# Forgetting attention and a SwiGLU block: q and k of the first three batches through GpSimd's DMA queue with a cast on the way

## The chip, the cores and the metric

The kernel runs on one core of a Trainium2 chip. The time is that of one execution on the device, in microseconds (us); lower is better. Each core has TensorE (PE in the profile; its weight loads are PEld), VectorE (DVE), ScalarE (ACT), GpSimd (POOL) and SyncE (SP), and DMA queues that the engines issue into. TensorE's results land in PSUM, of which there are eight banks, and are read from there by DVE or ACT.

## What is computed

Eight batches, eight heads, 576 tokens, head size 64; then a feed-forward block over all 4608 tokens (model width 512, inner width 1536).

```python
scores = scale * np.matmul(q, k.transpose(0, 1, 3, 2))
cum = np.cumsum(np.log(np.clip(f, 0.0001, 1.0)), axis=-1)
scores = np.where(causal, -1000000000.0, scores + cum[:, :, :, None] - cum[:, :, None, :])
attn = softmax(scores)                                  # over the last axis
x = np.matmul(attn, v)                                  # (B, H, S, D) -> (B*S, H*D)
g = x @ w_gate
out = (g * sigmoid(g) * (x @ w_val)) @ w_out
```

All inputs and the output are float32; the kernel computes its matmuls in bfloat16.

## The kernel before

**Attention.** Two heads make a pair, four pairs a batch. `QK` holds, for eight pairs at a time, q and k turned so that the head's 64 channels lie on partitions 0 to 63 and the tokens along the row; four further partitions hold the decay in parts, so that one matmul of 68 rows gives scores with decay. For each head, `score` writes four groups of score columns to PSUM (the first of them, i = 0, needs only tokens 0 to 255), `expo` takes the exponential on ACT, `mask` zeroes the upper triangle on GpSimd, `weigh` multiplies by v on TensorE, `invert` and `scale` normalise on DVE, `flip` and `put` turn the result into `xT`, the feed-forward block's input.

**Feed-forward block.** For each tile of tokens, 12 inner blocks: `gate` with `wg`, tanh on ACT, two DVE operations, `gate` with `wv` between them, then `project` with `wo`. Batch 0's 576 tokens are two tiles (256 and 320), the rest are tiles of 512.

**Loads before the change.** v comes by SyncE in float32 and is cast, mostly on GpSimd. The weights come by GpSimd with a cast to bfloat16 in the transfer, 384 columns (or three inner blocks) at a time: `weights`, L708 for gate and value, L705 for out. For q and k there are three ways:

- Batch 0, `first_queries` (L500): SyncE loads float32 in two token halves (0 to 255, then 256 to 575; L473), TensorE turns them in float32 against a float32 identity (`turn_x`, L485), ACT and DVE copy them into `QK` with the cast (`straighten_x`).
- Batches 1 and 2, `queries` (L521): SyncE loads 96 partitions of 2 heads x 6 tokens (L408) into unused places of `xT`, or of `wo` for pairs 4 and 5; `cast_qk` casts them into one of four `BF` buffers on ACT, DVE or GpSimd; `turn` (L418) turns one token of both heads at a time, 128 columns of `BF`, whose last 32 partitions are zero; `straighten` copies into `QK`.
- Batches 3 to 7: `narrow` casts q and k from memory to memory by GpSimd, and SyncE's transposing DMA (L435) brings them into `QK`.

**Decay.** f is loaded on ACT's queue in two parts; for each part clip, Ln, a running sum and four scaled remainders follow (L314 to L334), and `row` (L352) moves them into `QK`'s decay rows by SyncE's queue.

**Order of the work.** A planner (`Plan.run`, L66) runs once when the program is built. Each operation has a key, an earliest time, needs and an estimated cost; the planner plays the engines forward and emits, on each, the ready operation with the lowest key. The result is a fixed order per engine: at run time each engine takes its instructions in that order and waits at each for what it needs. The constants at the end of the file (`W_AT`, `Q1_AT`, `KEY_X`, ...) shift these keys and earliest times. Where the planner sees TensorE idle between 2 and 40 us with a free bank, it puts in a filler matmul (`dummy`, L813) whose result nobody reads. Score and turn results can borrow the feed-forward block's four banks until `BORROW`.

Helpers record many operations under one line: L295 is a copy or cast on ACT, L297 one on DVE or GpSimd, L337 a fill.

Of the kernel before, what the change touches and what calls it, by code (L numbers as in the profile page):

```python
# [23 lines left out]
class Op:  # L24
    def __init__(self, eng, fn, after, take, use, key, ready, dma, late):
        self.eng, self.fn, self.take, self.use = eng, fn, take, take + use
        self.key, self.ready, self.dma, self.late = key, ready, dma, late
        self.after = [a for a in after if a is not None]
        self.next, self.wait = [], 0
        self.start = self.done = None  # L30


class Plan:
# [9 lines left out]
    def op(self, eng, fn, after=(), take=(), use=(), key=0.0, ready=0.0, dma=None, late=0.0):  # L43
        o = Op(eng, fn, list(after), list(take), list(use), key, ready, dma, late)
        for b in o.use:
            b.left += 1
        self.ops.append(o)
        return o
# [17 lines left out]
    def run(self, idle=None):  # L66
# [12 lines left out]

        def push(at, kind, o):  # L80
            nonlocal seq
            seq += 1
            heapq.heappush(events, (at, seq, kind, o))
# [4 lines left out]
        while left:  # L88
# [4 lines left out]
            while events and events[0][0] <= t + 1e-9:  # L93
                _, _, kind, o = heapq.heappop(events)
                if kind in ("queue", "dma"):
                    busy_rings = [r for r in rings.values() if r]
                    for r in busy_rings:
                        r[0][0] -= (t - moved) * (0.6 if len(busy_rings) > 1 else 1.0)
                        while r and r[0][0] < 1e-6:
                            over, n = r.pop(0)  # L100
                            if r:
                                r[0][0] += over
                            n.done = t + 1.0
                            push(n.done, "end", n)
                            push(n.done + n.late, "done", (n, None, False))
                    moved = t
                    if kind == "queue":
                        rings["POOL" if o.ran == "POOL" else "HW"].append([o.dma, o])
                    busy_rings = [r for r in rings.values() if r]
                    if busy_rings:  # L110
                        push(t + min(r[0][0] for r in busy_rings) / (0.6 if len(busy_rings) > 1 else 1.0), "dma", None)
# [80 lines left out]
def kernel(ctx, tc, q, k, v, f, w_gate, w_val, w_out, out):  # L192
# [39 lines left out]
    BF = [sb(f"BF{i}", [P, QT, 2, D], BF16) for i in range(4)]  # L232
# [13 lines left out]
    def part(r):  # L246
        return wo[:, KF // 4 * r : KF // 4 * (r + 1)].rearrange("p a b -> p (a b)")

    lf, zero, cum, r1 = [xT[:BH, r, : 2 * S].bitcast(F32) for r in range(4)]
    dec = [xT[:BH, r, N_TOK - 2 * S :].rearrange("p (w s) -> p w s", w=2) for r in range(4)]  # L250
    nat = {"nat": [xT[:QP, r, N_TOK - 2 * S - 4 * QT * D : N_TOK - 2 * S].bitcast(F32).rearrange("p (h x) -> p h x", h=2) for r in range(KD)],
           "natw": [part(r)[:QP].bitcast(F32).rearrange("p (h x) -> p h x", h=2) for r in range(4)]}

    TX, PX = (2, 4), (HALF // 2, (S - HALF) // 4)
    natx = [[OT[r].rearrange("p (h x y) -> p x h y", h=2, x=2) for r in range(FB)],
            [xT[: PX[1], r, N_TOK - 2 * S - 8 * TX[1] * D : N_TOK - 2 * S].bitcast(F32).rearrange("p (h x y) -> p x h y", h=2, x=2) for r in range(FB)]]
    ident32 = consts.tile([P, P], F32, name="ident32")
# [3 lines left out]
        {"f": 4, "s": 2, "o": 1, "t": 1, "pt0": NPT0, "pt": NPT, "vb": NVB, "nv": NNV, "nat": KD, "natw": 4, "bf": 4,  # L261
# [78 lines left out]
    o_one = op(("POOL", 0.1), fill, warm, 1.0, key=-20)  # L340
    o_wln = op(("ACT", 1.5), lambda e: nc.scalar.activation(warm, warm, AF.Ln), after=[o_one], key=-18)
    o_id = op(("POOL", 0.8), lambda e: make_identity(nc, ident[:, :]), key=-19)
    o_zero = op(("DVE", 0.55), fill, zero, 0.0, key=-18)
    o_dec = [op(("DVE", 0.25), fill, dec[r][:, 0 if r else 1], 1.0, key=-17) for r in range(4)]
    o_i32 = op(("DVE", 0.4), lambda e: nc.vector.tensor_copy(ident32, ident), after=[o_id], key=-16)
    o_bf = [op(("POOL", 0.75), lambda e, i: fill(e, BF[i][QP:], 0.0), i, key=60, ready=22.0) for i in range(4)]

    def row(e, r, c):
        n = (FB, FIRST * FB)[c]
        for p0, p1, x in ((0, FB, CUTS[c]),) if c == 0 else ((0, FB, CUTS[c]), (FB, FIRST * FB, slice(0, S))):  # L350
            if p0 < p1:
                E[e].dma_start(  # L352
                    out=QK[D + r : D + r + 1, p0:p1, :, x].rearrange("o b (j w) s -> o (b j) w s", w=2),
                    in_=dec[r][2 * p0 : 2 * p1, :, x],
                )
# [3 lines left out]
    for c in range(2):  # L359
        x, kc, d = CUTS[c], (-15, CHAIN)[c], (256, 320)[c] / 960  # L360
        o = op(("DVE", 0.15 + d), clip, c, after=[o_f[c]], key=-16)
        o = op(("ACT", 0.2 + d), log, c, after=[o, o_wln], key=-16)
# [8 lines left out]
        o_row.append([op((ROWQ[c], (0.5, 0.9)[c] if FIRST > 1 else 0.5), row, r, c, after=[a, o_dec[r]] + o_chain[r : 4 * c : 4], key=ROW_KEY[c] + r,  # L371
                         dma=0.2) for r, a in enumerate((o_up, o_hi, o_mid, o_lo))])
# [19 lines left out]
    o_warm = op(("ACT", 1.4), lambda e: nc.scalar.activation(warm, lf[:1, :1], AF.Exp), after=[o_ln], key=-14)  # L392
# [14 lines left out]
    def ld_qk(e, p, nm, b):  # L407
        nc.sync.dma_start(out=nat[b.pool][b.i], in_=srcs[nm][2 * p : 2 * p + 2].rearrange("h (p t) d -> p h (t d)", t=QT))  # L408

    def cast_qk(e, bn, bb):  # L410
        dst, src = BF[bb.i][:QP].rearrange("p t h d -> p h t d"), nat[bn.pool][bn.i].rearrange("p h (t d) -> p h t d", d=D)
        copy(e, dst, src)

    def turn(e, bb, bt):
        src = BF[bb.i].rearrange("p t h d -> p t (h d)")
        t = ps(bt).bitcast(BF16)
        for n in range(QT):
            nc.tensor.transpose(t[:, n * QP : n * QP + P], src[:, n], ident)  # L418

    def straighten(e, p, x, a, bt):  # L420
        dst = QK[:D, hqk[p].i, 2 * a + x, :S].rearrange("p (c n) -> p c n", n=QT)
        src = ps(bt).bitcast(BF16)[a * D : (a + 1) * D, :S].rearrange("p (n c) -> p c n", n=QT)
# [30 lines left out]
    def values(b, n, key, after=(), ready=0.0):  # L453
        bv = Buf("nv")
        o = op(("SP", SPi), ld_v, b, n, bv, take=[bv], key=key, dma=1.6 if n < NB - 1 else 0.8, after=after,
               ready=ready, late=LATE if b >= FIRST else 0.0, tag=("ldv", b, n))
# [10 lines left out]
    a_ready, x_turned = {}, []  # L467
    prev_narrow = {}
    wo_free = []

    def ld_x(e, p, nm, x, half):
        n, lo = TX[half], HALF * half
        nc.sync.dma_start(  # L473
            out=natx[half][p][:, x],
            in_=srcs[nm][2 * p : 2 * p + 2, lo : lo + n * PX[half]].rearrange("h (p t) d -> p h (t d)", t=n),
        )

    def turn_x(e, p, half, xs, bt):
        m = PX[half]
        c = 0  # L480
        for x in xs:
            for h in range(2):
                for y in range(TX[half] // 2):
                    o = ps(bt)[:, c : c + TX[half] // 2 * m].rearrange("p (n y) -> p y n", y=TX[half] // 2)[:, y]
                    nc.tensor.transpose(o, natx[half][p][:, x, h, P * y : P * y + P], ident32[:m, :m])  # L485
                c += TX[half] // 2 * m

    def straighten_x(e, p, half, xs, t, bt):
        n, lo = TX[half] // 2 * PX[half], HALF * half
        q = QK[:D, p, :, lo : lo + 2 * n]  # L490
        src = ps(bt)[t * D : (t + 1) * D, : len(xs) * 2 * n]
        if half:
            dst = q[:, xs[0] :: 2].rearrange("p h (n t) -> p h n t", t=2)[:, :, :, t]
            src = src.rearrange("p (h n) -> p h n", h=2)
        else:
            dst = q.rearrange("p (h x) (n t) -> p x h n t", x=2, t=2)[:, :, :, :, t]
            src = src.rearrange("p (x h n) -> p x h n", x=2, h=2)
        copy(e, dst, src)

    def first_queries(p):  # L500
        strs = []
        for half in range(2):
            key = KEY_X[half] + 5 * p
            lds = [op(("SP", SPi), ld_x, p, nm, x, half, key=KEY_L[half] + 5 * p + x, dma=(0.67, 0.71)[half], ready=X_AT[half],
                      tag=("ldx", p, half)) for x, nm in enumerate("qk")]
            for xs in ([0, 1],) if half == 0 else ([0], [1]):
                bt = Buf("t", ("f", 30.0), ("s", 12.0))
                o3 = op(("PE", 4 * (0.15, 0.1)[half]), turn_x, p, half, xs, bt, after=[lds[x] for x in xs] + [o_i32], take=[bt],
                        key=key, tag=("turnx", p, half))
                x_turned.append(o3)  # L510
                for t in range(2):
                    strs.append(op({"ACT": (0.7, 0.5)[half], "DVE": (0.7, 0.5)[half]}, straighten_x, p, half, xs, t, bt,
                                   after=[o3] + strs[:1], take=[] if strs else [hqk[p]],
                                   use=[bt] + ([hqk[p]] if strs else []), key=key, tag=("strx", p, half)))
            for j in range(2):
                if half:
                    q_ready[2 * p + j] = strs + o_row[0] + o_row[1]
                else:
                    a_ready[2 * p + j] = strs + o_row[0]
# [354 lines left out]
```

The softmax here doesn't subtract the row's maximum and nothing guards it: scores larger than these inputs give would overflow.

## Time and profile before

| | |
|---|---|
| median of 4 runs | 407.27 us (407.2 to 407.58) |
| the profiled execution, its own time | 406.87 us |
| its span, first to last instruction | 405.2 us |
| TensorE busy | 392.5 us, 97% |
| TensorE weight loads | 232.0 us, 57% |
| DVE busy | 230.8 us, 57% |
| ACT busy | 225.1 us, 56% |
| GpSimd busy | 128.9 us, 32% |
| SyncE's DMA queue (q1), GpSimd's (q0) | 38.8 MB and 10.6 MB, 46.7% and 16.6% of the DMA engines' span |
| read from memory, written | 38.3 MB, 15.8 MB |

Times inside the profile count from the span's start. A busy TensorE is not TensorE at its best: matmuls overlap, their ends are modelled, and the clock may be reduced (PEclk, 1.00 is full). A DMA share over 1 comes from packets of two queues that overlap on one DMA engine. The chain of waits follows the work that ended last back to what released it, so a long DMA entry in it is a time in which the end of the kernel waited for that load.

### The profile page before, as it was taken

What the parts mean: (1) busy time and instruction counts of PE and PEld (TensorE: products, weight loads), DVE (VectorE), ACT (ScalarE), POOL (GpSimd) and SP (SyncE); (2) the same over time, 40 slices, a digit from 0 to 9 for tenths busy, and PEclk for the clock granted to TensorE, in tenths of its full rate; (3) what the DMA queues carried; (4) which work ended last, traced back from release to release, by engine and by line L of the source; (5) the groups of instructions that cost most, each with busy time, mean ns of one, the idle gap of its engine ahead of it and who ended that gap; (6) DMA issues with size and microseconds to landing.
All of it is one profiled execution on the core that took longest, in us unless ns stands there. A gap on an engine that the chain in (4) does not pass through costs nothing.

```text
span 405.2 us, 8557 instructions
## 1 busy us (share of the span) xinstructions
PE 392.5 (97%) x3166; PEld 232.0 (57%) x3211; DVE 230.8 (57%) x452; ACT 225.1 (56%) x457; POOL 128.9 (32%) x357
## 2 busy tenths in 40 slices
PE   8979999999999999999999999999999999999996
PEld 6748878655554555556556555565664444444542
DVE  7525988646772477337643675267743761770850
ACT  6558978747762665466636665566763322322321
POOL 4938655443350333234415432533330000000000
PEclk9979999999999999999999999999999999999999
DMA  8999999047952985899699879975202002002002
GB/s 201 185 216 217 223 228 211 30 148 173 184 96 81 193 163 112 151 196 163 105 156 196 154 138 148 146 155 119 48 28 79 0 2 104 0 2 103 2 10 82
DMA packets 105818, 50.12 MB, mean 124 GB/s; under 512 B 87920, under 2 KB 100656, under 8 KB 105456
## 3 DMA queue, kind: packets, MB, share of 16 engines
q1 hardware_dynamic: 99312, 38.80, 46.7%
q0 software_dynamic: 6304, 10.62, 16.6%
q8 instruction: 25, 0.41, 0.4%
q10 hardware_dynamic: 160, 0.15, 0.2%
q14 instruction: 17, 0.14, 0.1%
HBM read 38.34 MB, written 15.78 MB: 134 GB/s over the span
## 4 chain that ended last, share of the span: by engine, by line
PE 86%; DMA 7%; SPq 3%; DVE 2%; issue 1%; ACT 1%; ACTq 0%; DVEq 0%
PE ps L712 42%; PE ps L727 23%; PE ps L580 10%; PE ps L611 7%; DMA xT<-in_k_dram 4%; SPq L435 2%; DMA QK<-dec_d 2%; PE ps L635 2%; PE ps L418 1%; DMA xT<-in_f_dram 1%; DVE QK L297 0%; PE ps L813 0%; SPq L352 0%; DVE xT L321 0%; DVE xT L328 0%
## 5 line engine op out<-in xcount | busy, mean ns | idle before, releaser
L712 PE MATMUL ps<-xT,wv 128*128 128x512 bf16 (+3 forms) x467 | 111.9, 358 | 0.8
L712 PE MATMUL ps<-xT,wg 128*128 128x512 bf16 (+3 forms) x465 | 111.5, 359 | 0.7
L716 ACT ACTIVATE th<-ps 128x512 f32<-128x512 f32 (+3 forms) x120 | 66.5, 555 | 72.3 <-PE ps L712 70.7
L588 ACT ACTIVATE PT<-ps 128x384 bf16<-128x384 f32 (+2 forms) x192 | 93.0, 507 | 23.9 <-PE ps L580 14.1
L720 DVE SCALAR_TENSOR_TENSOR th<-th,ps 128x512 f32<-128x512 f32 (+3 forms) x120 | 75.5, 629 | 53.4 <-ACT th L716 53.0
L727 PE MATMUL ps<-wo,hh 128*128 128x512 bf16 (+1 forms) x427 | 104.3, 379 | 0.9
L723 DVE TENSOR_TENSOR hh<-th,ps 128x512 bf16<-128x512 f32 (+3 forms) x120 | 76.1, 634 | 14.6 <-PE ps L712 2.8
L597 POOL TENSOR_SCALAR_AFFINE_SELECT PT<-PT 128x128 bf16<-128x128 bf16 (+1 forms) x192 | 53.1, 279 | 83.3 <-ACT PT L588 78.2
L580 PE MATMUL ps<-QK 68*128 68x320 bf16 (+4 forms) x448 | 72.5, 263 | 1.6 <-DMA QK<-xT 1.0
L712 PEld LDWEIGHTS <-wv 128*128 128x128 bf16 x480 | 45.1, 98 | 35.7 <-issue 0.4
L727 PEld LDWEIGHTS <-hh 128*128 128x128 bf16 (+1 forms) x444 | 41.8, 98 | 41.4 <-issue 1.2
L712 PEld LDWEIGHTS <-wg 128*128 128x128 bf16 x480 | 45.1, 98 | 35.3
L597 POOL TENSOR_SCALAR_AFFINE_SELECT PTa<-PTa 128x256 bf16<-128x256 bf16 x64 | 25.7, 410 | 82.4 <-ACT PTa L588 76.3
L731 ACT ACTIVATE ot<-ps 128x512 f32<-128x512 f32 (+1 forms) x37 | 22.1, 597 | 51.5 <-PE ps L727 51.3
L618 DVE RECIPROCAL rc<-ps 128x5 f32<-128x5 f32 (+2 forms) x64 | 12.3, 191 | 63.7 <-PE ps L611 63.3
L611 PEld LDWEIGHTS <-PT 128*128 128x128 bf16 x768 | 38.3, 97 | 17.7 <-POOL PT L597 1.1
L611 PE MATMUL ps<-VB,PT 128*128 128x65 bf16 x768 | 45.4, 193 | 0.1
L580 PEld LDWEIGHTS <-QK 68*128 68x128 bf16 x448 | 34.8, 98 | 12.3 <-issue 1.8
L588 ACT ACTIVATE PTa<-ps 128x384 bf16<-128x384 f32 x64 | 30.7, 491 | 15.8 <-PE ps L580 15.6
L625 DVE TENSOR_TENSOR xn<-ps,rc 128x320 bf16<-128x320 f32 x56 | 27.5, 491 | 1.8
L295 ACT ACTIVATE QK<-ps 64x576 bf16<-64x576 bf16 (+2 forms) x31 | 19.3, 628 | 9.7 <-DVE QK L297 7.9
L297 POOL CAST VB<-natv 128x512 bf16<-128x512 f32 (+1 forms) x38 | 23.2, 620 | 4.7 <-DMA natv<-in_v_dram 4.7
(54 smaller groups left out, 196.8 us busy)
## 6 DMA issues: line engine op xcount, KB each, us to landing
out_dram<-ot SPq DMA_DIRECT2D x35, 256.0 KB
natv<-in_v_dram SPq DMA_DIRECT2D x32, 256.0 KB
qk_d<-in_q_dram POOLq DMA_DIRECT2D x5, 576.0 KB, 6.2
qk_d<-in_k_dram POOLq DMA_DIRECT2D x5, 576.0 KB, 9.6
xT<-in_q_dram SPq DMA_DIRECT2D x6, 288.0 KB
xT<-in_k_dram SPq DMA_DIRECT2D x6, 288.0 KB
wg<-in_moe_w_gate_dram POOLq DMA_DIRECT2D x4, 384.0 KB, 9.9
wv<-in_moe_w_val_dram POOLq DMA_DIRECT2D x4, 384.0 KB, 11.5
```

Source lines behind the costliest of these rows:

```text
L297: E[e].tensor_copy(dst, src)
L580: nc.tensor.matmul(s[:, c : c + w], QK[:KR, hqk[p].i, 2 * j + 1, kt * P : (kt + 1) * P], QK[:KR, hqk[p].i, 2 * j, q0 : q0 + w], start=True ...
L588: nc.scalar.activation(place(h, i)[:, OFFS[i] : OFFS[i] + c], ps(bs)[:, :c], AF.Exp, scale=0.125)
L597: nc.gpsimd.affine_select(out=d, in_=d, pattern=pat, compare_op=ALU.is_ge, fill=0.0, base=0, channel_multiplier=-1,)
L611: nc.tensor.matmul(o[:, lo : lo + D + 1], pt[:, c : c + P], VB[hvb[b].i][:, kt, hb, : D + 1], start=first and n == 0, stop=last and n == l ...
L625: nc.vector.tensor_mul(XN[bx.i][:, qb : qb + nq, j], o, r)
L712: nc.tensor.matmul(ps(bf)[:, :n], w[:, ko, fc * P : (fc + 1) * P], xT[:, ko, t0 : t0 + n], start=(ko == 0), stop=(ko == KD - 1))
L716: nc.scalar.activation(TH[bt.i][:, :n], ps(bf)[:, :n], AF.Tanh, scale=0.5)
L720: nc.vector.scalar_tensor_tensor(out=t, in0=t, scalar=1.0, in1=ps(bf)[:, :n], op0=ALU.add, op1=ALU.mult)
L723: nc.vector.tensor_mul(HH[:, bh.i, lo : lo + n], TH[bt.i][:, :n], ps(bf)[:, :n])
L727: nc.tensor.matmul(ps(bf)[:m, :DM], HH[:, hs[fc].i, lo : lo + m], wo[:, fc, :], start=(fc == 0), stop=(fc == KF - 1))
L731: nc.scalar.activation(OT[bo.i][:m], ps(bf)[:m, :DM], AF.Copy, scale=0.5)
```

## The change

All 24 tensors-of-a-pair of batches 0 to 2 (q and k of 12 pairs) are loaded by GpSimd's queue, cast to bfloat16 in the transfer, 96 partitions of 2 heads x 6 tokens each. `first_queries`, its two token halves, the float32 identity, `cast_qk` and the `BF` buffers go. `turn` now takes two neighbouring tokens of one head at a time: 96 partitions of 128 columns, six per tensor, straight from the loaded tile. There are eight places in `xT` and eight in `wo`; batch 1 uses those in `wo`, so all of `w_out`'s loads now wait for batch 1's last turn. `row` is cut into three steps (batch 0's first part, batch 0's second part, batch 1). The planner's picture of the two DMA rings is refined (a starting GpSimd ring takes nearly all), its costs of loads are changed, and the constants at the end of the file are new, which moves many instructions on every engine. In the built program the number of fillers goes from 95 to 59. On GpSimd's queue the eight loads of batch 0 stand ahead of the first six weight transfers.

```diff
 class Op:
-    def __init__(self, eng, fn, after, take, use, key, ready, dma, late):
+    def __init__(self, eng, fn, after, take, use, key, ready, dma, late, pk):
+        self.pk = pk
...
+        def share(busy):
+            if rings["POOL"] and rings["POOL"][0][1] is None:
+                return [1.0 if r is rings["POOL"] else 0.1 for r in busy]
+            return [0.6, 0.65] if len(busy) > 1 else [1.0]
...
                     if kind == "queue":
-                        rings["POOL" if o.ran == "POOL" else "HW"].append([o.dma, o])
+                        r = rings["POOL" if o.ran == "POOL" else "HW"]
+                        if o.ran == "POOL" and not r:
+                            r.append([1.5, None])
+                        r.append([o.dma, o])
...
-    BF = [sb(f"BF{i}", [P, QT, 2, D], BF16) for i in range(4)]
...
+    def places(t, lo, n):
+        return [t[:QP, lo + i * 2 * QT * D : lo + (i + 1) * 2 * QT * D].rearrange("p (h t) -> p h t", h=2) for i in range(n)]
+
+    nat = {"nat": [a for r in range(KD) for a in places(xT[:, r], N_TOK - 2 * S - 4 * QT * D, 2)],
+           "natw": places(wo.rearrange("p a b -> p (a b)"), 0, 8)}
...
-    o_one = op(("POOL", 0.1), fill, warm, 1.0, key=-20)
+    o_one = op(("DVE", 0.1), fill, warm, 1.0, key=-20)
-    o_id = op(("POOL", 0.8), lambda e: make_identity(nc, ident[:, :]), key=-19)
+    o_id = op(("POOL", 0.8), lambda e: make_identity(nc, ident[:, :]), key=KEY_Q + 3.5)
-    o_i32 = op(("DVE", 0.4), lambda e: nc.vector.tensor_copy(ident32, ident), after=[o_id], key=-16)
-    o_bf = [op(("POOL", 0.75), lambda e, i: fill(e, BF[i][QP:], 0.0), i, key=60, ready=22.0) for i in range(4)]
...
     def ld_qk(e, p, nm, b):
-        nc.sync.dma_start(out=nat[b.pool][b.i], in_=srcs[nm][2 * p : 2 * p + 2].rearrange("h (p t) d -> p h (t d)", t=QT))
-
-    def cast_qk(e, bn, bb):
-        dst, src = BF[bb.i][:QP].rearrange("p t h d -> p h t d"), nat[bn.pool][bn.i].rearrange("p h (t d) -> p h t d", d=D)
-        copy(e, dst, src)
-
-    def turn(e, bb, bt):
-        src = BF[bb.i].rearrange("p t h d -> p t (h d)")
-        t = ps(bt).bitcast(BF16)
-        for n in range(QT):
-            nc.tensor.transpose(t[:, n * QP : n * QP + P], src[:, n], ident)
+        nc.gpsimd.dma_start(out=nat[b.pool][b.i], in_=srcs[nm][2 * p : 2 * p + 2].rearrange("h (p t) d -> p h (t d)", t=QT))
+
+    def turn(e, bn, bt):
+        src, t, n = nat[bn.pool][bn.i], ps(bt).bitcast(BF16), 0
+        for h in range(2):
+            for y in range(QT // 2):
+                nc.tensor.transpose(t[:, n : n + QP], src[:, h, P * y : P * y + P], ident[:QP, :QP])
+                n += QP
 
     def straighten(e, p, x, a, bt):
-        dst = QK[:D, hqk[p].i, 2 * a + x, :S].rearrange("p (c n) -> p c n", n=QT)
-        src = ps(bt).bitcast(BF16)[a * D : (a + 1) * D, :S].rearrange("p (n c) -> p c n", n=QT)
+        dst = QK[:D, hqk[p].i, x::2, :S].rearrange("p h (n y t) -> p h n y t", n=QP, t=2)[:, :, :, :, a]
+        src = ps(bt).bitcast(BF16)[a * D : (a + 1) * D, :2 * S // 2].rearrange("p (h y n) -> p h n y", h=2, n=QP)
         copy(e, dst, src)
...
                 kk = key + 2 * x
-                o1 = op(("SP", SPi), ld_qk, p, nm, bn, take=[bn], key=kk, dma=1.1, after=x_turned,
-                        ready=max(ready, release(p) - SLACK) + 0.9 * x,
-                        tag=("ldqk", p))
-                o2 = op(copier(QT * 2 * D, False), cast_qk, bn, bb,
-                        after=[o1] + o_bf, take=[bb], use=[bn], key=kk, tag=("cast", p))
-                if p in WPAIRS:
-                    wo_free.append(o2)
-                o3 = op(("PE", mm(*[P] * QT)), turn, bb, bt, after=[o2, o_id], take=[bt], use=[bb], key=kk,
-                        tag=("turn", p))
+                o1 = op(("POOL", 0.35), ld_qk, p, nm, bn, take=[bn], key=kk, dma=0.74,
+                        ready=max(ready, release(p) - SLACK) + 0.3 * x, tag=("ldqk", p), late=(0.0, LATE0, LATE)[b])
+                o3 = op(("PE", mm(*[QP] * QT)), turn, bn, bt, after=[o1, o_id], take=[bt], use=[bn], key=kk, tag=("turn", p))
+                if b == 1:
+                    wo_free.append(o3)
...
     for p in range(FB):
-        first_queries(p)
+        queries(p, KEY_Q + 4 * p)
...
-W_AT = [9.0, 14.5, 11.3, 31.6]
-WO_AT = [35.2, 23.3, 56.0, 39.0]
-Q1_AT = [12.3, 35.1, 34.2, 53.1]
-V1_AT = 34.2
-CHAIN = 16.8
+W_AT = [-2.8, -18.4, -0.5, 15.6]
+WO_AT = [28.1, 28.3, 50.7, 57.5]
+Q1_AT = [24.1, 27.1, 27.5, 39.5]
+V1_AT = 28.1
+CHAIN = 30.6
...
-FREE = 128.1
+FREE = 87.7
...
-BORROW = 24.0
+BORROW = 33.9
+KEY_Q = -17.9
```

## The prediction, made before the changed kernel was run

> **What bounds the kernel now.** I read the busy shares first. TensorE is busy 97% of the span, and in the page's slices only the opening is visibly thin. Lines 1 and 2 of the page, then the stages of the opening (TensorE's busy time and count, granted clock, DMA share, GB/s):
>
> ```profile
> PE 392.5 (97%) x3166; PEld 232.0 (57%) x3211; DVE 230.8 (57%) x452; ACT 225.1 (56%) x457; POOL 128.9 (32%) x357
> PE   8979999999999999999999999999999999999996
> ...
> 15.00:20.00 5.00, 4.73 (x63) 1.00 1.24 239
> 20.00:25.00 5.00, 2.55 (x28) 0.98 1.34 206
> 25.00:30.00 5.00, 4.43 (x24) 0.50 1.24 232
> 30.00:35.00 5.00, 5.00 (x44) 0.83 1.12 201
> 35.00:40.00 5.00, 5.00 (x79) 1.00 1.16 226
> ```
>
> Busy hides two things: fillers (L813, work that nobody needs) and a clock at half from about 24.8 to 31.7. So I used a ledger: the matmuls in instruction order, each at its issue interval, fillers and early turns (L485) left out. The intervals come from runs of equal matmuls: four of 512 columns in 0.86 us give 0.216 each, other widths in proportion, nothing under 0.055; 24 products P·V (L611) in 0.89 us give 0.037. The whole kernel comes to 377.8 us. What the clock shows beyond the ledger is TensorE's loss so far. The chain of waits gives the clock at each mark:
>
> ```profile
> 13.38 8.57 DMA xT<-in_k_dram
> 21.96 5.84 DMA xT<-in_k_dram
> 27.94 0.78 PE ps L485 x4
> 29.93 2.29 PE ps L712 x12
> ...
> 72.17 0.65 PE ps L727 x3
> ```
>
> First gate (L712, start 28.77): ledger 4.4, loss 24.4. First turn of batch 1 (L418, 37.98): ledger 10.8, loss 27.2. First projection (72.17): ledger 45.1, loss 27.1. End (405.2): 377.8, loss 27.4. **So everything TensorE loses is lost before 38 us; the other 367 us are dense.** The loss is made by the two long waits above: SyncE's loads of batch 0's second token half, in flight beside the weights, keep the last turns of pairs 2 and 3 back, and behind them, in order, all other TensorE work.
>
> **What the Trainium skill says.** "DMA: Bandwidth & Descriptors", Queues, rings and completion order: all queues share 16 engines, each of which goes round-robin between queues, packet by packet. The trace agrees: a 160 KB load took 8.57 us from issue to landing beside weights. The same page, SWDGE vs HWDGE vs iDMA: a cast in the transfer can only be issued by GpSimd, which writes the descriptors itself. So each load costs GpSimd time; the trace has 0.53 us for a two-index load and 0.77 to 1.07 for weights. "TensorE: Matmul & The Clock Gate", Part 1: the clock goes to half after an idle window of about 3.4 us and comes back after a busy one. The trace agrees roughly: half clock for 6.8 us after a stage only 51% busy.
>
> **The change, part by part.**
> *Removed.* 16 casts (8 on DVE at 0.55 to 0.65, 2 on ACT at 0.84, 6 on GpSimd at 0.82: 11 us over three engines), four zero fills of 0.73 on GpSimd, GpSimd's two decay scalings (0.94 and 1.14, now on ACT at an estimated 0.45, like its Ln), 32 SyncE issues of about 0.46. None lies on TensorE's dense path; they count only in the opening.
> *TensorE.* 96 turns of 128 columns become 144 of 96, at 0.055 each: +2.6 us in the ledger, now 380.4. They include batch 0's, which the 48 float32 turns did before (outside the ledger, in idle time).
> *Data.* 24 loads of 288 KB (144 KB written) go through GpSimd's queue. The packet records show 192-packet transfers costing what weights cost per packet: 512 weight packets moved in 2.0 us alone, so 0.76 each. Batch 0's eight stand ahead of the weights in the same ring, so nothing of the weights can delay them; that is the core of the change. A first weight packet moved 1.7 us after the issue began, and a starting ring moved 126 packets per us: first load 2.5, five loads (pairs 0, 1 and q of pair 2, all that stands before the first score) by about 10, eight by 13, six weight transfers by 25, the last two by 29. SyncE keeps only v and the decay rows; rows of batch 0 are issued from about 6.3 to 9.6 (before 7.1 to 10.35).
> *First score.* Two issues, a fill and the identity put TensorE's first filler at 3.2 (before 1.46). By the fillers' own spacing the clock became full 6.3 us after the first one; say 9.5. In the order 48 fillers (0.23 cold, 0.11 warm) and 30 turns precede the first score: about 22 fillers and 12 turns cold, 26 × 0.11 + 18 × 0.06 + 0.1 = 4.0 warm: 13.5 us. Before: 14.96. First exponential 13.9.
> *ACT then sets the pace.* Almost all of batch 0's attention now precedes the FFN. Before the gate stand, in ACT's order, 8 early exponentials (0.491), heads 0 to 4 (0.597 + 0.488 + 0.437 = 1.52 each), two of head 5 and 3 straightenings (0.644): 3.9 + 7.6 + 1.1 + 1.9 = 14.6. 28.5, plus mask and product: first gate about 29.4, no earlier than before. But the ledger there is 12.7, not 4.4. Batch 0's last exponential ends 18.4 us after the first, 32.3; its last product stands at ledger 15.9 and runs at about 33.5: loss 17.6.
> *After that.* From first to 24th tanh, ACT's operations sum to 32.9 us and DVE's to 33.6, against 37.3 in the ledger: TensorE leads again. Before, ACT was 84 to 88% busy in 30 to 70 us and TensorE lost nothing. I add 1.1 for small waits: loss 18.7.
> *Late next.* Batch 1's turns come at 17.7 + 18.7 = 36.4 and later; their loads are issued from about 26 and land at about 30: hidden by 5 us. w_out is issued behind batch 1's last turn, 34.5 + 18.7 = 53.2, and GpSimd waits there with the masks behind it; the exponentials for those come later in the order too. Three issues by 55.6, a fourth at about 58; landing took 8.0 to 11.0 before: 66 to 69, against the first projection at 50.7 + 18.7 = 69.4. Hidden, with little to spare; up to 2 us if not.
> *Sum.* 380.4 + 18.7 = 399.1 of span, against 405.2. The profiled execution took 406.87, 1.67 more than its span, and the median of the runs is 0.40 above that: 401.2, say **401.3 us**.
>
> **Unknown costs, both ends.** A 192-packet load on GpSimd: 0.53 (nearest row) to 1.07 (longest issue seen); taken 0.55. At 0.8 the ten before the gate add 2.5 to GpSimd's 27 us and make it the pacer. A 96-row turn: 0.04 (columns alone) to 0.083 (busy time each of L418's): -1.4 to +2.7 us over batches 1 and 2; taken 0.055. The first use of GpSimd's queue at 0.8 instead of 9.5 us: the first issue took 0.2 longer than the next; I take nothing, with 0 to 2 us as bounds, and 2 us earlier never helps since ACT paces. A fuller ring: before, five weight transfers were issued ahead of the first landing without a stall; now 14 could be issued by 12.6, and a stall would cost 0 to 2.
>
> **Rivals.**
> *B, part of it is given back:* GpSimd's issues at 0.8, or w_out late, cost 2 to 5 us: 403 to 406, say 404.5. For it: GpSimd has 27 us of work before the gate that waits for it at 29. Against: masks of neighbouring heads overlap in the trace.
> *C, hidden anyway:* the later loads and their transposes (DMA 80 to 90% busy in many slices to 280 us) hold TensorE to its old times: no change, 407.3. Against: zero loss from 38 us on.
> *D, slower, by the clock:* from 14 to 29 TensorE has 10 us of ledger in 15.5, 65%, with no fillers after the first products, where the filler-padded stage before it was 95% busy. If the clock drops for the attention stage, 10 becomes 20 us (gate at 34) and the recovery costs what it cost before, 6.8 at half, 3.4: 8 us on top, 409. It decides at 6.1 us lost, or 12.2 us of dense work at half clock. Against: the drop in the trace followed 51% busy with whole idle microseconds; here gaps are fractions of one.
> That the change doesn't do what it says is no rival: in the built order the 24 loads stand on GpSimd, bf16, before the weights.
>
> **How the numbers follow.** Forecast A 0.60 (own range 398.5 to 404), B 0.17, C 0.05, D 0.13, anything else slower 0.05. A change of 0.2% (0.8 us) is about what a measurement of this kernel can tell from none. Faster: A and B, 0.77. Same: C and B's edge, 0.06. Slower: D and the rest, 0.17. Low end 397.5: A with 0.04 turns and first gate 1 us earlier. High end 408.5: B, C and a milder D, leaving about 0.1 above.
>
> **What would show it.** Right: no load of k in the chain of waits after 15 us; first score near 13.5, first gate near 29.4 but with batch 0's attention nearly done; ACT close to 100% from 14 to 31; clock full in 20 to 35; dense TensorE from 34; first projection near 69. Wrong: first score after 16, half clock after 15, GpSimd without idle before the gate or issues of 0.8 and more, TensorE waiting for w_out or for batch 1's loads.

## The result: no change, and where the profile puts the time

The changed kernel takes 407.5 us in the median (36 runs), the kernel before, run beside it, 407.2 us (55 runs). The ratio is 1.0001, with a 95% interval from 0.9986 to 1.0015: no difference that can be measured, where 401.3 us and a faster kernel had been forecast. Some executions are several us longer at a lower granted clock; all ratios leave these out, and so are not quite the quotients of the medians. The profiled execution of the changed kernel took 406.62 us, its span 404.6 us (before: 406.87 and 405.2).

The page of the changed kernel, TensorE's busy time, its 40 slices and its granted clock:

```profile
PE 383.9 (95%) x3130; PEld 225.1 (56%) x3175; DVE 230.4 (57%) x444; ACT 220.7 (55%) x448; POOL 133.2 (33%) x369
PE   5659999999999999999999999999999999999996
PEclk9959999999999999999999999999999999999999
```

The same stages of the opening as were shown of the kernel before (stage, then length, TensorE's busy time and count, granted clock, DMA share, GB/s):

```profile
15.00:20.00 5.00, 3.38 (x45) 1.00 1.27 193
20.00:25.00 5.00, 0.42 (x7) 0.62 1.29 192
25.00:30.00 5.00, 5.00 (x43) 0.50 1.27 196
30.00:35.00 5.00, 4.85 (x79) 0.85 1.34 179
35.00:40.00 5.00, 4.37 (x60) 1.00 1.29 224
```

The emptiest stage, 20 to 25 us, has become emptier (2.55 to 0.42 us of work), and a half clock is still there, now from 21.2 to 31.5 us. TensorE's waits from 12 to 45 us (engine, line and tile, what it waited for: us in all, times, longest) and the chain of waits name what is late:

```profile
PE ps L528 <- DMA QK<-xT: 6.3, 2, 4.6
```

```profile
14.02 10.72 DMA QK<-xT
24.74 0.14 issue
24.88 1.55 PE ps L528 x8
```

The two long waits for `xT<-in_k_dram` are gone. In their place stands one wait of 10.72 us for `QK<-xT`: the decay rows of batch 0's second token part, tiny transfers on SyncE's queue, issued by `row` (L354) at about 14 us and landed at 24.74. The timeline shows that they were not alone (start, length, engine and line, operation; the bracket gives the idle time before and what ended it):

```profile
10.08 0.73 SPq L443 DMA_DIRECT2D natv<-in_v_dram  x1
10.91 1.51 SPq L354 DMA_DIRECT2D QK<-xT  x2
12.47 0.44 SPq L443 DMA_DIRECT2D natv<-in_v_dram  x1
13.00 2.43 SPq L354 DMA_DIRECT2D QK<-xT  x3
24.52 0.61 POOL L302 CAST VB<-natv 128x512 bf16<-128x512 f32 x1 [3.89 <-DMA natv<-in_v_dram]
24.88 1.55 PE L528 MATMUL ps<-QK 68*128 68x192 bf16 x8 [4.58 <-DMA QK<-xT]
```

v's blocks 4 and 3 of batch 0 (L443) were issued in between, at 10.1 and 12.5 us, and block 3 landed only at about 24.5: from issue to landing block 4 took over 8 us, the last row 10.7 and block 3 12. What moved in those ten microseconds, by queue (packets, MB, share of 16 engines; q0 is GpSimd's queue, q1 SyncE's):

```profile
q0 software_dynamic: 1933, 1.44, 92.1%
q1 hardware_dynamic: 1776, 0.48, 34.6%
```

A packet here is one record of the profile, one piece of a transfer. The two queues moved nearly one packet for one packet. A packet of GpSimd's loads writes 768 bytes, one of v 256. SyncE's queue got 178 packets, or 48 KB, per us. From 2 to 4 us, with almost nothing beside it, it had moved 1545 packets and 0.39 MB, 195 KB per us, its start included. Before the change the same ten microseconds had 836 packets of SyncE with 0.71 MB, because its loads of q and k came in packets of 1024 bytes. GpSimd's queue moved 2006 there, so equal counts are not seen in that kernel; SyncE's queue had gaps (62 packets from 20 to 23 us).

The first gate starts at 36.4 us (28.8 before), the first projection at 75.3 (71.2 before). From the first projection to the end it is 329.3 us, against 334.0 before: the dense part became shorter, since more of the attention is done ahead of it, but the opening became longer by 4.1, and the two nearly cancel: 0.6 us of span is left, less than the executions of one kernel differ by.

### The profile page after: what moved, and what is told of

It is laid out like the page before. It is cut to its first block, busy times and chain, and to the rows that moved or that the text cites. A ratio compares the mean times of both kernels' runs of the same rounds, so it can differ in the third digit from the quotient of the medians.

```text
span 404.6 us, 8424 instructions
## 1 busy us (share of the span) xinstructions
PE 383.9 (95%) x3130; PEld 225.1 (56%) x3175; DVE 230.4 (57%) x444; ACT 220.7 (55%) x448; POOL 133.2 (33%) x369
## 4 chain that ended last, share of the span: by engine, by line
PE 85%; DVE 6%; DMA 3%; issue 2%; ACT 2%; POOL 1%; SPq 0%; DVEq 0%; ACTq 0%; POOLq 0%
PE ps L660 42%; PE ps L675 23%; PE ps L528 10%; PE ps L559 7%; DMA QK<-xT 3%; DVE QK L302 2%; PE ps L583 2%; DVE hh L671 1%; DMA xT<-in_f_dram 1%; DVE th L668 1%; POOL wo L410 1%; ACT PT L536 1%; PE ps L416 1%; POOL PT L545 0%; DVE xT L326 0%
## 5 line engine op out<-in xcount | busy, mean ns | idle before, releaser
L660 PE MATMUL ps<-xT,wv 128*128 128x512 bf16 (+3 forms) x464 | 110.3, 357 | 0.6
L664 ACT ACTIVATE th<-ps 128x512 f32<-128x512 f32 (+3 forms) x120 | 66.6, 555 | 69.4 <-PE ps L660 67.9
L536 ACT ACTIVATE PT<-ps 128x512 bf16<-128x512 f32 (+2 forms) x192 | 91.9, 511 | 22.3 <-PE ps L528 12.8
L528 PE MATMUL ps<-QK 68*128 68x320 bf16 (+4 forms) x448 | 75.8, 267 | 7.5 <-DMA QK<-xT 6.3
L545 POOL TENSOR_SCALAR_AFFINE_SELECT PT<-PT 128x128 bf16<-128x128 bf16 (+1 forms) x192 | 52.2, 274 | 78.8 <-ACT PT L536 72.6
L559 PEld LDWEIGHTS <-PT 128*128 128x128 bf16 x768 | 40.4, 98 | 15.7 <-POOL PT L545 0.4
L559 PE MATMUL ps<-VB,PT 128*128 128x65 bf16 x768 | 48.3, 194 | 0.2
L302 DVE COPY QK<-ps 64x576 bf16<-64x576 bf16 x24 | 18.9, 798 | 13.8 <-PE ps L416 12.4
L302 DVE COPY xT<-ps 128x576 bf16<-128x576 bf16 (+2 forms) x34 | 14.5, 427 | 20.2 <-PE ps L583 20.2
## 6 DMA issues: line engine op xcount, KB each, us to landing
wg<-in_moe_w_gate_dram POOLq DMA_DIRECT2D x4, 384.0 KB, 12.5
wv<-in_moe_w_val_dram POOLq DMA_DIRECT2D x4, 384.0 KB, 12.5
```

Of the source, the lines that this page charges most:

```text
L302: E[e].tensor_copy(dst, src)
L528: nc.tensor.matmul(s[:, c : c + w], QK[:KR, hqk[p].i, 2 * j + 1, kt * P : (kt + 1) * P], QK[:KR, hqk[p].i, 2 * j, q0 : q0 + w], start=True ...
L536: nc.scalar.activation(place(h, i)[:, OFFS[i] : OFFS[i] + c], ps(bs)[:, :c], AF.Exp, scale=0.125)
L545: nc.gpsimd.affine_select(out=d, in_=d, pattern=pat, compare_op=ALU.is_ge, fill=0.0, base=0, channel_multiplier=-1,)
L559: nc.tensor.matmul(o[:, lo : lo + D + 1], pt[:, c : c + P], VB[hvb[b].i][:, kt, hb, : D + 1], start=first and n == 0, stop=last and n == l ...
L660: nc.tensor.matmul(ps(bf)[:, :n], w[:, ko, fc * P : (fc + 1) * P], xT[:, ko, t0 : t0 + n], start=(ko == 0), stop=(ko == KD - 1))
```

## The experiments

Every edit is made to the changed kernel, and every ratio is to the kernel before, run on the same chip. Not all experiments ran on the same chip as each other, so between them the ratios are the safer comparison. First all of them together (medians; the span, first gate and first projection are those of the profiled execution, which is the fastest of ten for v_long, at 400.27 us, and the slowest of six for v_early, at 404.09):

| kernel | us | ratio and 95% interval | span | first gate | first projection |
|---|---|---|---|---|---|
| changed | 407.5 | 1.0001 (0.9986 to 1.0015) | 404.6 | 36.4 | 75.3 |
| rows_act | 405.33 | 0.9948 (0.9926 to 0.997) | 404.1 | 36.5 | 75.1 |
| v_long | 402.3 | 0.9873 (0.984 to 0.9906) | 398.6 | 30.3 | 69.5 |
| fillers45 | 405.92 | 0.9961 (0.9942 to 0.998) | 403.6 | 34.9 | 74.3 |
| v_early | 402.55 | 0.9867 (0.9832 to 0.9902) | 402.2 | 34.0 | 72.9 |
| v_split | 406.89 | 0.9987 (0.9965 to 1.0009) | 404.9 | 36.7 | 75.7 |
| v_split_fill | 406.96 | 0.9986 (0.9965 to 1.0007) | 404.1 | 35.9 | 74.8 |
| weights_later4 | 407.2 | 0.9992 (0.9969 to 1.0014) | 406.3 | 35.9 | 77.0 |
| v_early_fill | 403.53 | 0.992 (0.9896 to 0.9944) | 401.8 | 33.1 | 72.5 |
| v_early_lo | 402.4 | 0.9882 (0.9854 to 0.991) | 401.1 | 29.2 | 71.8 |
| v_early_lo_fill | 402.86 | 0.9888 (0.986 to 0.9916) | 401.3 | 31.6 | 72.0 |
| v1_hold | 400.1 | 0.9805 (0.9765 to 0.9845) | 397.8 | 29.2 | 68.6 |

In every row, span less first projection is between 329.0 and 329.3 us. So the whole question lies ahead of the first projection.

**rows_act: the second decay rows on another queue.** ACT issues them instead of SyncE.

```diff
-        E[e].dma_start(
+        (nc.scalar if c == 1 else E[e]).dma_start(
```

> Edit: only the four decay-row transfers of batch 0's second part go from SyncE's queue to ACT's, so that no v load stands ahead of them in their queue. Theory T1 (turn-taking: SyncE's queue moves one packet for each packet of GpSimd's, and 1536 packets of 256 bytes of v stand ahead of the last rows): rows landed by about 17 instead of 24.8 and the 4.6 us wait of the scores for QK<-xT gone; but the cast of v's block 3, which waits for its load until 24.5 and has the masks behind it on GpSimd, is then late next, so the first gate comes only 0 to 2 us earlier and the time falls by 0 to 2 us. T2 (the engines are simply full, bytes ahead of the rows): the rows land at 22 or later. T3 (ACT and GpSimd pace the opening anyway): no change of time, and no engine idle by more than 1 us between 18 and 25.

The wait for the rows fell from 6.3 to 1.4 us, but the next thing on SyncE's queue took its place. TensorE's waits, then two pieces of the chain:

```profile
PE ps L559 <- POOL PTa L545: 4.2, 2, 3.1
PE ps L528 <- DMA QK<-xT: 1.4, 1, 1.4
```

```profile
10.84 13.95 DMA natv<-in_v_dram
...
24.84 0.61 POOL VB L302
```

GpSimd waits for v's block 3 with its cast (`VB`, L302), and its masks, which TensorE needs, stand behind that cast. The span fell by 0.5 us. So the rows were only the last to come in the wait: v's block 3 stands behind it on the same queue. The rows did not land by 17 either. With nothing of v ahead of them, the last one was issued at 15.12 and the scores that need it began at 20.77, so some 5 us of a row's landing are not explained by v.

**v_long: v's blocks 3 and 4 in long rows.** As many bytes, at the same place of the same queue, as 192 packets of 2048 bytes instead of 1536 of 256. They come from other tokens, so this kernel does not compute batch 0's attention; it shows the time alone.

```diff
+        if b == 0 and n > 2:
+            nc.sync.dma_start(out=natv[bv.i][:m].rearrange("p h d -> p (h d)"),
+                              in_=v[b].rearrange("h s d -> (h s d)")[: m * H * D].rearrange("(p x) -> p x", x=H * D))
+            return
```

> Edit: v's blocks 3 and 4 of batch 0 are loaded as 192 rows of 2048 bytes, with the same bytes in the same places of the queues, but taken from other tokens (so batch 0's output is not the reference's). T1: 192 packets instead of 1536 ahead of the last rows and of the casts; rows landed by about 17, no wait over 1 us for QK<-xT or v after 18, clock full from 20 to 35, first gate at 30 to 32 instead of 36.4, time 401 to 404. T2 (bytes): rows still at 22 to 25, time as before within 0.3%. T3: rows early, but the first gate still after 34 and the time within 0.3%.

Queues from 14 to 20 us, and the stage that had been empty:

```profile
DMA packets 1670, 1.39 MB, mean 232 GB/s; under 512 B 228, under 2 KB 1478, under 8 KB 1669
q0 software_dynamic: 1213, 0.90, 97.0%
q1 hardware_dynamic: 456, 0.48, 28.2%
```

```profile
20.00:25.00 5.00, 4.70 (x53) 0.74 1.27 193
```

SyncE's queue moved its 0.48 MB within 6 us instead of 10, in 456 packets instead of 1776. GpSimd's queue lost nothing by it: 202 packets per us, where it had 193 in the changed kernel. TensorE has 4.70 us of work where it had 0.42. With as many bytes in fewer packets SyncE's queue is through earlier, so its share beside GpSimd's follows the number of packets and not the bytes. The total rate also rose, from 193 to 232 GB/s, so short packets use the engines less well too; this run does not part the two. The median is 5.2 us under the changed kernel's. The profiled span of 398.6 is the fastest execution's, and that it lies near the 399.1 of the prediction says little. Not all of the expectation held: the last row landed at 19.2, 5.17 us after its issue, and not by 17, and the clock still fell to half for 3.4 us.

**fillers45: the clock alone.** 45 matmuls that nobody needs are put before the group of scores that waits, so that TensorE stays busy through the wait.

```diff
+        if (h, i) == (0, 1):
+            for _ in range(45):
+                nc.tensor.matmul(s[:, :HALF], ident, ident.unsqueeze(1).to_broadcast([P, 2, P]), start=True, stop=True)
```

> Edit: 45 filler matmuls in TensorE's order right before the score group that waits for the second decay rows, nothing else. It parts the wait from the clock that follows it. T1 as to the wait: the rows still land at about 24.8. If the half clock (21.2 to 31.4) costs what its dense part says, about 6.5 us of work at half, the time falls by 2 to 3.5 us (first gate about 33.5); if ACT or GpSimd pace that stage, the clock stays full but the time falls by less than 0.8 us.

```profile
20.00:25.00 5.00, 5.00 (x50) 1.00 1.29 191
```

The granted clock is full throughout, and the first gate comes 1.5 us earlier, the end 1.0 us. So the half clock follows from the idle wait and costs 1 to 1.5 us, less than expected. The wait itself stays.

**v_early: v's blocks 3 and 4 first.** SyncE issues them right behind blocks 0 to 2, ahead of all decay rows.

```diff
+        if (r, c) == (0, 0):
+            for n in (4, 3):
+                m = min(P, S - n * P)
+                nc.sync.dma_start(out=natv[{4: 3, 3: 4}[n]][:m], in_=v[0, :, n * P : n * P + m].rearrange("h p d -> p h d"))
```

> Edit: v's blocks 3 and 4 of batch 0 are issued right behind blocks 0 to 2, before the decay rows, in the 4 us in which SyncE otherwise waits for the decay; nothing else moves. T1: they pass before the weights reach the ring; no v load stands ahead of the second rows; rows landed by about 17, v cast without a wait, clock full, first gate 30 to 32, time 400 to 403.5. T2: the same bytes have to pass before the rows, so the first rows (14.6) come later by up to 1.5 us and the second rows gain less than 4; time 404 to 407. T3: within 0.3% of before.

1.3% faster than the kernel before. The chain of waits shows what remained:

```profile
5.04 6.49 DMA xT<-in_q_dram
...
16.76 0.89 DVE xT L339
...
17.67 4.82 DMA QK<-xT
```

GpSimd's loads of q and k are slower now that v's packets move beside them: 5.5 to 7.4 us from issue to landing, where the changed kernel had 4.5 to 5.3. Equal turns do not explain this: from 8 to 9 us SyncE's queue moved 530 packets and GpSimd's 34. What held these loads back stays open. And the last remainder of the decay (L339), behind straightenings on DVE, is ready only at 17.65. Its row then takes 4.82 us, and the queues from 17 to 21 us show no packet of SyncE at all:

```profile
q0 software_dynamic: 1068, 0.80, 129.8%
```

So about 5 us are what a row needs beside a full GpSimd queue, with v (10.72) or without (4.82 here, 5.17 in v_long), and by this estimate v's packets account for about half of the 10.72 us, which is more than TensorE's wait of 4.6. No run shows what makes up the other half. First gate 34.0, not the expected 30 to 32.

**v_split and v_split_fill: block 4 early, block 3 behind the second rows**; the second kernel adds 20 fillers as in fillers45.

```diff
+        if (r, c) == (0, 0):
+            block(4)
...
+        if (r, c) == (3, 1):
+            block(3)
```

> Edit: of batch 0's v, block 4 (512 packets) is issued right behind blocks 0 to 2, block 3 (1024 packets) behind the second decay rows. T1, with what the earlier runs showed: putting both blocks early made a q load wait (11.5)[...]; here only 512 packets stand before the q and k loads and none before the second rows. Rows landed by 18, first score below 15, first gate 30 to 33, time 400.5 to 402.5. If what is left is the rows' own slow landing, no better than with both blocks early (402.5).

> Edit: as v_split, with 20 filler matmuls right before the first score group of the second rows. If the clock still drops after that wait, fillers keep it full and save 0.5 to 1.5 us against v_split; if it no longer drops there, they cost nothing or up to 1 us.

Neither is measurably faster than the kernel before, which was not expected. The chain, and the timeline of GpSimd:

```profile
15.35 10.01 DMA natv<-in_v_dram
```

```profile
25.41 0.61 POOL L302 CAST VB<-natv 128x512 bf16<-128x512 f32 x1 [6.12 <-DMA natv<-in_v_dram]
```

Block 3, 1024 packets, took 10.0 us here, 12 in the changed kernel and 13.95 with block 4 before it in rows_act: long wherever it was issued while GpSimd's queue was full. It was needed as much as the rows. Of what was tried here, two things helped: longer packets, and issuing it before that queue fills.

**weights_later4: GpSimd's queue made emptier.** Four weight transfers (the second and third part of gate and value) are issued only behind the third mask.

```diff
+        masks[0] += 1
+        if masks[0] == 4:
+            for w in held:
+                tc.no_sync_barrier()
+                send(*w)
```

> Edit: four of the six weight transfers that stand behind batch 0's q and k in the ring (the second and third pieces of gate and value) are issued only after the third mask on GpSimd, behind the fourth pieces. v and the rows keep their places. T1: GpSimd's ring runs empty near 17.5, SyncE's queue then moves alone, rows landed by about 19 instead of 24.8 and v's cast with them; first gate 31 to 34, time 402 to 405.5, the upper part if 3 us of issues now stand between the masks. T2 (total bytes before the first gate): no better than 406.5, since all the same bytes must pass.

GpSimd's queue ran empty as intended, and SyncE's queue then went four times as fast, with the same 256-byte packets of v. The queues from 17 to 19 us:

```profile
q1 hardware_dynamic: 1570, 0.42, 109.7%
q0 software_dynamic: 92, 0.06, 19.7%
```

That is 785 packets per us, where the changed kernel had 178 beside the weights. But the time is that of the kernel before. v's block 3 landed at 21.2 us instead of 24.5, and five weight issues of about 0.75 us (the four and one more, 21.8 to 25.5) then stood before GpSimd's masks, and the loads of pair 4 came late behind the weights. From the chain:

```profile
33.08 11.99 DMA wo<-in_k_dram
```

What one stage gained was lost in the next, where a load took 12 us from issue to landing (3.4 to 7.4 us in the changed kernel).

**v_early_fill, v_early_lo, v_early_lo_fill: what was left in v_early.** All three are v_early with something added. v_early_lo computes the last two remainders of the second decay part on DVE right behind the step they follow from, ahead of the straightenings; v_early_fill adds 25 fillers to v_early, and v_early_lo_fill 15 to v_early_lo, as in fillers45.

```diff
+        if x == CUTS[1]:
+            nc.vector.tensor_scalar_mul(dec[2][:, 1, x], r1[:, x], 1.0)
+            nc.vector.tensor_sub(dec[3][:, 1, x], r1[:, x], dec[2][:, 1, x])
```

> Edit: as v_early, with 25 fillers right before the first score group of the second rows, which there still waited until 22.6 and had the clock at half from 22.1 to 29.0. The same clock step as in the changed kernel (where fillers took 1.5 us off): clock full from 22 on, time 0.5 to 2 us under v_early, 400.5 to 402.

> Edit: as v_early, and DVE computes the last two remainders of the decay's second part before the straightenings of q and k instead of behind four of them (in v_early the last remainder ended at 17.6, since a straightening waited for a late q load). If what was left of the wait is the late issue of the last row: rows issued by 13 and landed by 17, score group without a wait, clock full after 20, first gate 31 to 32.5, time 399.5 to 401.5. If it is the rows' slow landing behind the two queues: landed no earlier than 20, time within 0.8 us of v_early (402.5).

> Edit: as v_early_lo, with 15 fillers before that score group. Theory: with the rows early the wait is gone, so the fillers have no wait to fill and cost 0 to 1.6 us against v_early_lo, unless the clock still drops, when they save up to 1 us.

In v_early_lo the first gate came at 29.2, 4.8 us earlier than in v_early, and yet the end came only 1.1 us earlier and the median is the same. The waits of TensorE say why:

```profile
PE ps L425 <- DMA wo<-in_q_dram: 2.1, 1, 2.1
PE ps L425 <- DMA xT<-in_q_dram: 1.1, 1, 1.1
```

The second line is a load of batch 0, early in the opening. The first is new: the turns of batch 1 (pair 4, in `wo`) wait for their loads. These were issued at 26.6 and 27.2 and landed 11 to 12 us later: another stall had been lying behind the first one. The fillers gave nothing in either kernel (ratios 0.992 beside 0.9867, 0.9888 beside 0.9882), though the clock was full with them.

**v1_hold: the same cause, one batch later.** v_early_lo, and in it v's blocks of batch 1, with the decay rows behind the first of them, wait on SyncE until GpSimd has issued batch 1's first six loads. A tiny fill on GpSimd makes them wait.

```diff
+        if b == 1 and not first:
+            first.append(n)
+            nc.gpsimd.memset(natv[bv.i][:, 0, :1], 0.0)
         nc.sync.dma_start(out=natv[bv.i][:m], in_=v[b, :, n * P : n * P + m].rearrange("h p d -> p h d"))
```

> On top of v_early_lo, SyncE's v blocks of batch 1 (and the decay rows of batch 1 behind the first of them) are held until GpSimd has issued the first six loads of batch 1: a tiny fill on GpSimd behind them writes the first block's buffer (it stands at about 32.4 us; v_early_lo issued these blocks from 16.7 on). In v_early_lo the first gate came at 29.2, as predicted for the change, but pair 4's q and k, issued at 26.6 and 27.2, landed after 37.9 and 38.9, and TensorE waited for them. Theory 1 (turn-taking): the 256-byte packets of batch 1's v held these loads back; without them pair 4 lands within 5 to 8 us of its issue, by 33 to 35, TensorE does not wait for it, first gate stays near 29.2, span 398.5 to 399.7, time 400 to 401.3. Theory 2 (order in the ring): the loads are late because of the weight transfers ahead of them on GpSimd's own queue; then pair 4 still lands at 37 to 39 and the time stays at 402.4. Loss to watch: GpSimd's casts of batch 1's v now wait until about 37 to 39, and no mask is due before 43.8, so that should cost nothing.

The loads into `wo`, from issue to landing, in v_early_lo and then in v1_hold:

```profile
DMA to landing us min/median/max: 4.0/11.4/11.7
```

```profile
DMA to landing us min/median/max: 3.6/5.1/5.4
```

And the queues from 27 to 32 us, v_early_lo and then v1_hold:

```profile
q0 software_dynamic: 943, 0.70, 89.7%
q1 hardware_dynamic: 946, 0.24, 36.3%
```

```profile
q0 software_dynamic: 1272, 0.93, 124.1%
```

943 packets against 946 again; without SyncE's, 1272 of GpSimd's. The weights ahead of these loads in GpSimd's own queue are the same in both kernels, so they were not what made them late. Pair 4's loads land at about 32 us instead of 38 to 39, and no wait for them is left. The first projection starts at 68.6, the median is 400.1 us: **2.0% faster than the kernel before (0.9805, 0.9765 to 0.9845).** It keeps everything that the change did; what it adds is the order of SyncE's queue, the tiny fill, and the place of two DVE steps. The same order was not tried on the kernel before, so the 2.0% belongs to the change and the order together.

## Why the prediction was wrong, step by step

**The step that failed is "Data".** It said that batch 0's eight loads stand ahead of the weights in one ring, "so nothing of the weights can delay them; that is the core of the change", and that "SyncE keeps only v and the decay rows". The first half was right. The second was left without a price: what SyncE's queue would get beside GpSimd's. The prediction had cited the Trainium skill, "DMA: Bandwidth & Descriptors", Queues, rings and completion order, for engines that go round-robin between queues by packet, but applied it only to q and k beside the weights. (The one number that it gave for it, 8.57 us for a load beside weights, fits that but counts no packets.) Applied to what stays on SyncE's queue, it would have asked for the packets: v's blocks 3 and 4 are 1536, and GpSimd's ring, the list of its transfers still to be moved, is never empty before they are through. In bytes they are 0.39 MB, 2 us at the 195 KB per us that SyncE's queue moved alone; at the measured 178 packets per us they take 8.6 us (an estimate), and the rows share that queue. Their first packets moved at about 14 us, so that gives 22.6 at the earliest, where TensorE came to the scores that need the rows at 20.3. The last row landed at 24.74. The sum has no term for TensorE's wait for it, nor for the masks' wait behind v's block 3.

**The working's other steps, in order.**
- *Ledger.* Right. From the first projection to the end it gave 380.4 - 50.7 = 329.7 us; 329.0 to 329.3 were measured in all twelve versions of the changed kernel. For the kernel before it gave 332.7, and 334.0 were measured from the first projection's start at 71.2; the 72.17 of the chain, used as the mark, is a later piece of the same group. Of the 2.6 us for turns of 96 columns only batch 2's half lies behind the first projection and so within this agreement; neither half was measured alone.
- *Loss.* The end was at 380.4 + 24.2, not 380.4 + 18.7. These 5.5 us are the error in the span. By the ledger, the change won 3.2 us against the 27.4 lost before, and paid 2.6 for turns.
- *First score 13.5.* It came at 14.63, after 1.75 us of waiting for the first decay rows. The first filler ran at 4.25 instead of 3.2. One GpSimd issue took 0.63 to 0.66 us, not 0.55. v1_hold has its first score at 14.70, 1.2 later than forecast, and still its first gate at 29.2: the stage between took 1.4 us less than the sum had it. That these two errors cancel is luck.
- *ACT then sets the pace, first gate 29.4.* As a pace it is right once SyncE's queue is not starved; the figure came out (29.2 in v1_hold) by the luck just named. ACT's busy time from 20 to 26 us, in the changed kernel and then in v1_hold:

```profile
20.00:26.00 6.00, 0.00 (x0) 0.60 1.28 192
```

```profile
20.00:26.00 6.00, 5.94 (x16) 1.00 1.31 203
```

- *Late next.* Batch 1's loads were taken as landing at about 30, hidden by 5 us. In v_early_lo pair 4's landed at 38 to 39: the same unpriced queue. `w_out`, which was put down as hidden with little to spare, was: no wait of TensorE for it shows up to 80 us in v1_hold.
- *Sum.* With both faults of SyncE's order taken away, span 397.8 and first projection 68.6 stand beside the worked-out 399.1 and 69.4 (v1_hold's profiled execution is the fastest of six; its median, 400.1, stands beside 401.3). The gain that was forecast is there to be had; the order on a queue that the sum had not priced kept it from coming.

**The rivals.** C's figure (407.3) came true, its reason did not: in all twelve versions the end followed the first projection by 329.0 to 329.3 us, so nothing later held TensorE to its old times. D's half clock did come, from 21.2 to 31.5 us, but with 4.6 us of idle waiting and not from small gaps, and fillers45 puts it at 1 to 1.5 us, not 8. Of B a part was there: GpSimd's issues for batch 1 stand in the chain of waits with 3.0 us between 33 and 39 us, in part in front of masks; what they cost was not measured alone. In weights_later4 such issues took back what had been won. The rival that was missing is SyncE's queue: 1536 short packets, and behind them something that TensorE needs before GpSimd's ring runs dry.

## What to carry to other kernels

When a load is moved to another queue, count the packets of everything that stays. Here v's short packets beside GpSimd's busy queue moved at about that queue's packet rate, some 190 per us, so their bytes alone did not say when they would be through. Send short-packet loads before the other queue fills or after it is done with what is urgent, and keep tiny urgent transfers from standing behind them. And judge an opening by when the first dense work starts, for each version: a wait that is taken away may uncover another, as between v_early and v1_hold, and what the change can give shows only when both are gone.

## What the runs showed that had not been expected

- Beside SyncE's short packets GpSimd's queue fell only from 254 packets per us (1272 in 5 us) to 189 (943 in 5 us), a quarter less, while SyncE's fell from about 770 (1545 in 2 us) to 178, to less than a quarter. Equal numbers of packets are far from an equal loss.
- The Trainium skill, on the same page and section, has an engine drain a whole packet, typically of some 9 to 17 descriptors, before it switches. In the records here the 256-byte pieces of v and the pieces of GpSimd's loads move in nearly equal numbers (1776 to 1933, 946 to 943). That fits turns of single pieces, and also turns of equal bundles; the counts do not tell which.
- An issue can itself be long: with SyncE's queue occupied, one v block in v_early_lo took 5.97 us to issue, where 0.43 is usual, and all that stands behind it on SyncE waits. That the queue was full is inferred from this.
